# Six transpositions of x with float32r operands, from raw copies made by DMA within SBUF

## The chip, the cores and the metric

The kernel runs on one core of one Trainium2 chip. The metric is the device time of one execution in microseconds (us), the median of several executions; lower is better. The core has a matrix engine (PE, with its weight loads shown apart as PEld), three engines for element-wise work (DVE, ACT, POOL) and SP, which here issues all DMAs. Each engine works through its own queue in order and waits on semaphores for the others.

## What is computed

Three layers, in float32, for a batch of 2, a sequence of 768 and a width of 512 (8 heads of 64):

```
attn = softmax over keys of the same hash bucket of (q k^T / 8), times v     # 2 x 8 heads
x    = attn, heads side by side                                              # (2, 768, 512)
theta = x @ w_theta
y  = w_tok_r . (x cos(theta)) + w_tok_i . (x sin(theta))                     # over the sequence
u  = x + y
x  = u + relu(u @ w_ch)
out = x + relu(layernorm(x) g @ w_ch1) @ w_ch2
```

## The kernel before, in words

Every float32 product is made of float32r products: an operand is split into a high part (a cast to float32r) and a low part (the rest), and three of the four products of parts are added in PSUM.

The attention runs as 48 steps, two blocks of 128 queries each. A step ends with `pv_mm` (the product with v, line 405, tile `o`), `pv_evac_a` (ACT, line 414, tile `ot`) and `pv_evac_b` (DVE, line 423), which writes the transposed x: `XT[b]`, a tile per batch (b = 0, 1) with the width on partitions, 128 partitions by 4 by 768 words. In the listings these three are `PV`, `O` and `X`; the last of them is `X.47`. The pool of tiles that the attention used, `ap_`, is closed after it, and its place in SBUF is taken by one large tile, `arena` (128 partitions by 10 slots of 2,048 words).

The second layer works on twelve blocks of 128 tokens, named by batch b and block j. For a block, `z_h` and `z_l` split x (tiles `xh`, `xl`), `z_m` multiplies it with the split w_theta (line 790, tile `th`), `z_a` to `z_f` make cosine and sine, `z_t` transposes x back to tokens on partitions and `z_u` (ACT, line 776) takes that out of PSUM into `U`, `z_p` multiplies it with cosine and sine, and `z_q` and `z_w` split the products into `z_o[b, j]`. For j over 0, `z_o[b, j]` is slot 2j - 2 + b of `arena`, so slots 8 and 9 are those of block 5. `mix_mm` (line 856, tile `acc`) multiplies the token weights (`tokh`, `tokl`) with these, six products per step.

`z_t` (line 773, tile `xps`) is four transpositions on PE: each loads a 128 by 128 block of `XT[b]` as weights and streams the identity `ident`, both float32.

From line 505 on the order of every engine's queue is the order of the program (`manual_schedule`), and the program is written out by hand as lists of steps: `tail` (the end of the attention with the start of the second layer), then `half1`, `trans` and the rounds of the third layer. A step's arguments are numbers: `z_t.0.5.1` is block (0, 5) into PSUM bank T1, `mix.2.0` is product step 2 of batch 0, `ld.t.3.0` and `ld.c.0.1` are loads of token weights and of w_ch, issued on SP (line 106, tile `st`). The place that matters here is the end of `tail` and the start of `half1`:

```
    tail = ... PV.47 z_u.1.0 z_h.1.1 cv_y.t.1.1 z_t.1.1.1
        mix.0.0 O.47 z_r.1.0 z_u.1.1 cv_l.t.1.0.1 z_p.0.1.0 X.47
    half1 = z_u.1.3 z_c.1.0.1 z_q.0.1.0 z_f.1.0.0 z_f.1.0.1 ld.c.0.1 z_l.1.1 z_f.1.0.2 z_t.0.5.1
        mix.2.0 ... z_m.1.1.2 z_w.1.0.1.0 z_t.0.2.1 ...

    run(tail)
    actx.close()
    zq = zctx.enter_context(tc.tile_pool(name="z", bufs=1, side="right", reuse_waits="tile"))
    arena.append(zq.tile([128, 2 * NI - 2, 2048], F32R, name="arena"))
    run(half1)
```

On PE the six products of `mix.0.0` are followed at once by the four transpositions of `z_t.0.5.1`; on SP the last DMA ahead of `half1` is `ld.t.3.1`; `z_q.0.1.0` (ACT, a cast at line 94) is the first instruction that writes `arena`, into slot 0.

Of the kernel before, what the change touches and what calls it, by code (L numbers as in the profile page):

```python
# [10 lines left out]
F32R = mybir.dt.float32r  # L11
# [22 lines left out]
def attn_moe_kernel(  # L34
# [28 lines left out]
    vec, act, pool, pe, sp = nc.vector, nc.scalar, nc.gpsimd, nc.tensor, nc.sync  # L63

    def f(ap):
        return ap.bitcast(F32)
# [4 lines left out]
    def bank(tag, name):  # L71
        return psum.tile([128, 512], F32, tag=tag, name=name)
# [6 lines left out]
    ident = const.tile([128, 128], F32, name="ident")  # L79
# [8 lines left out]
    XT = {}  # L88
# [497 lines left out]
    for i in range(8):  # L586
        c, x = divmod(i, 2)
# [145 lines left out]
    def U(i):  # L733
        if i not in U_AT:
            return U0[:, i if i < 4 else i - 2, :]
        j, y = U_AT[i]
        if j not in ur:
            ur[j] = r_new(j, F32, f"u{j}")
        return ur[j][:, y, :]
# [4 lines left out]
    arena = []  # L744
# [8 lines left out]
    zb, zr, zw = {}, {}, {}  # L753
# [16 lines left out]
    def z_t(b, j, k):  # L770
        zb[b, j] = bank(f"T{k}", f"xps{b}{j}")
        for d in range(4):
            pe.transpose(zb[b, j][:, d * 128:(d + 1) * 128], XT[b][:, d, j * 128:(j + 1) * 128], ident)

    def z_u(b, j):
        act.activation(U(b * NI + j), zb.pop((b, j)), AF.Copy)

# [70 lines left out]
    def mix_mm(half, j, t, b):  # L848
        if j == 0 and t != 1:
            mix_acc(half, t, b)  # L850
        th, tl = tok_t[half, j]
        acc, z = acc_t[half, b, t], z_o[b, j]
        k = 0
        for x in range(2):
            for w, y in ((th, 0), (th, 1), (tl, 0)):
                pe.matmul(  # L856
                    acc, w[:, x, t * 128:(t + 1) * 128], z[:, x, y, :],
                    start=(j == 0 and k == 0), stop=(j == NI - 1 and k == 5),
                )
                k += 1  # L860
# [333 lines left out]
    def o_add(r, t, x0=None):  # L1194
# [6 lines left out]


    ops.update(
        z_tab=z_tab, z_h=z_h, z_l=z_l, z_t=z_t, z_u=z_u, z_m=z_m, z_a=z_a, z_k=z_k, z_r=z_r, z_c=z_c, z_f=z_f, z_p=z_p, z_q=z_q,
        z_w=z_w, mix=lambda q, b: mix_mm(q // 18, q % 18 // TH, q % TH, b), madd=mix_add, ch_new=ch_new, ch_at=ch_at, ch_ah=ch_ah, ch_al=ch_al, ch_bm=ch_bm,
        ch_br=ch_br, ch_bs=ch_bs, ln_a=ln_a, ln_b=ln_b, ln_c=ln_c, xb_new=xb_new, xn=xn_make, xb_t=xb_t, xb_e=xb_e,
        xb_a=xb_a, xb_h=xb_h, xb_l=xb_l, ld=cv_ld, cv_y=cv_y, cv_s=cv_s, cv_b=cv_b, cv_p=cv_p, cv_j=cv_j, cv_h=cv_h, cv_l=cv_l, w1_s=w1_s,
# [3 lines left out]
    def run(text, **names):  # L1211
# [15 lines left out]
    """  # L1227

    half1 = """
        z_u.1.3 z_c.1.0.1 z_q.0.1.0 z_f.1.0.0 z_f.1.0.1 ld.c.0.1 z_l.1.1 z_f.1.0.2 z_t.0.5.1  # L1230
        mix.2.0 cv_b.t.1.1 z_w.0.1.0.0 z_u.0.5 cv_h.t.1.1 z_p.1.0.1 z_p.1.0.0 z_q.1.0.1 cv_l.t.1.1.0 z_q.1.0.0
        z_q.0.1.1 cv_y.t.2.1 z_m.1.1.2 z_w.1.0.1.0 z_t.0.2.1 z_w.1.0.0.0 z_w.0.1.1.1 z_a.1.1 z_a.0.2 z_u.0.2
        z_k.1.1.0 cv_y.t.2.0
        mix.1.0 z_k.0.2.0 z_r.1.1 cv_s.t.2.0.1 z_m.0.3.1 z_c.1.1.1 z_r.0.2 z_f.1.1.1 cv_b.t.2.1 z_f.1.1.0
        z_h.1.2
# [3 lines left out]
        mix.4.0 z_p.0.2.0  # L1239
        mix.1.1 z_w.1.1.0.0 z_h.1.3 cv_s.t.3.0.1 z_q.1.1.1 z_a.0.3 z_m.1.2.2 cv_s.t.3.1.1 z_w.1.1.1.0 z_q.0.2.0  # L1240
        z_f.0.2.1 cv_h.t.2.0 z_p.0.2.1
        mix.3.1 z_q.0.2.1 cv_h.t.2.1 z_k.0.3.0 z_h.0.4 z_w.0.2.0.0 z_r.0.3 z_t.0.3.1 z_w.0.2.1.1 z_a.1.2
        z_c.0.3.0 ld.t.4.1
        mix.5.1 z_f.0.3.1 z_k.1.2.0 cv_l.t.2.1.0 z_r.1.2 cv_l.t.2.0.1 z_l.1.3 z_f.0.3.0 z_t.1.2.2
        mix.4.1
        mix.7.0 z_u.0.3 cv_y.t.3.0 z_p.0.3.1 z_u.1.2 z_c.1.2.0 cv_y.t.3.1 z_f.1.2.1 z_m.1.3.1
        mix.3.0 ld.t.4.0 cv_b.t.3.0 z_f.1.2.0 z_q.0.3.1 cv_b.t.3.1 z_l.0.4 z_f.0.3.2 z_f.1.2.2 z_p.1.2.1
# [7 lines left out]
        z_p.0.4.0 ld.t.5.1 z_q.1.3.0  # L1255
        mix.11.0 z_w.1.3.1.0 z_q.0.4.0 z_w.1.3.0.0 cv_h.t.4.0 z_a.1.4 z_w.0.4.0.1 z_k.1.4.0 z_f.0.4.1
        cv_h.t.4.1
        mix.11.1 z_p.0.4.1 z_r.1.4 z_q.0.4.1 z_t.1.4.2 cv_l.t.4.0.1 cv_y.t.5.0 cv_l.t.4.1.0 z_w.0.4.1.0 z_a.0.5
        z_h.1.5 ld.c.1.1 z_c.1.4.1
        mix.9.1 z_l.1.5 z_k.0.5.0 cv_s.t.5.0.1  # L1260
        mix.9.0 cv_s.t.5.1.1 z_r.0.5 z_u.1.4 z_f.1.4.0 cv_b.t.5.0 cv_y.t.5.1
        mix.10.1 ld.t.6.0
        mix.10.0 z_c.0.5.0 z_f.1.4.2 z_p.1.4.0 z_f.1.4.1 z_p.1.4.1 z_f.0.5.0 z_q.1.4.0 z_f.0.5.1 z_q.1.4.1
        cv_b.t.5.1 cv_h.t.5.0 ld.t.6.1 z_p.0.5.1 z_w.1.4.0.0 z_f.0.5.2 z_m.1.5.1 z_w.1.4.1.0 z_p.0.5.0
        mix.12.0 cv_h.t.5.1 z_q.0.5.1 z_t.1.5.2 z_a.1.5 cv_l.t.5.0.1 z_w.0.5.1.0 z_k.1.5.0 cv_l.t.5.1.0 z_r.1.5
        mix.12.1 cv_s.t.6.1.1 cv_y.t.6.0 z_q.0.5.0 cv_s.t.6.0.1 z_c.1.5.0 z_u.1.5 cv_y.t.6.1 cv_b.t.6.1
        mix.13.1 z_f.1.5.1 z_f.1.5.0
        mix.14.0
# [150 lines left out]
    for r in range(3, len(rounds)):  # L1419
        g = rounds[r][0] + r % 2  # L1420
        n = g + 1
        a, b, c, d = (
            (f" ld.v.{n}.0 ld.v.{n}.1", f" cv_y.v.{n}.0 cv_s.v.{n}.0.1", f" cv_p.v.{n}.0", f" cv_j.v.{n}.0") if n < NG else ("", "", "", "")
        )
# [59 lines left out]
```

## Time and profile before

| | |
|---|---|
| median of 3 runs | 663.49 us (663.41, 663.49, 665.45) |
| span of the profiled execution, first to last instruction | 662.6 us |
| PE busy | 657.1 us (99%), 3771 matmuls |
| DVE, ACT, POOL busy | 557.5, 416.4, 310.5 us |
| granted TensorE clock, mean | 1.000 |

The profile is of one execution. What it has of that execution's time is the span, which lies 0.9 us below the median; the rest lies around the first and the last instruction. A busy PE is counted from the start of a matmul to its modelled end, which overlaps the next one; the time that a matmul takes from its neighbours is read from start to start, or from the chain of waits, which cuts overlaps off.

### The profile page before, as it was taken

How to read it: one execution, taken by the hardware profiler on the slowest of the kernel's cores; microseconds unless marked ns; L12 is line 12 of the kernel's file. 1: busy time of each engine (PE TensorE's matmuls, PEld its weight loads, DVE VectorE, ACT ScalarE, POOL GpSimd, SP SyncE). 2: the span in 40 equal slices, each digit the busy share in tenths (PEclk: the TensorE clock that was granted, in tenths of full speed). 3: DMA queues.
4: the chain of work that ended last, by engine and by line, in shares of the span. 5: the costliest groups of instructions: out<-in, count | busy, mean ns of one | idle time of the engine just before them, and what ended most of it. 6: DMA issues, size and time to landing. Idle time of an engine off the chain costs nothing.

```text
span 662.6 us, 11210 instructions
## 1 busy us (share of the span) xinstructions
PE 657.1 (99%) x3771; PEld 591.7 (89%) x3771; DVE 557.5 (84%) x1002; ACT 416.4 (63%) x864; POOL 310.5 (47%) x418
## 2 busy tenths in 40 slices
PE   9999999999999999999999999999999999999998
PEld 7999999999999888888888888989998999999997
DVE  6899988999999999999888889986767686867655
ACT  7899998999999896776535544553433433343321
POOL 5887887667787644233433133434150505051400
PEclk9999999999999999999999999999999999999999
DMA  8977544475540411222422122102121121211022
GB/s 248 240 176 173 135 108 114 116 172 128 127 96 0 161 51 61 80 75 95 148 81 64 48 96 65 63 1 64 64 65 66 62 96 33 97 49 46 1 80 111
DMA packets 32374, 62.24 MB, mean 94 GB/s; under 512 B 4482, under 2 KB 11732, under 8 KB 32317
## 3 DMA queue, kind: packets, MB, share of 16 engines
q1 hardware_dynamic: 32317, 61.53, 33.1%
q8 instruction: 30, 0.49, 0.3%
q14 instruction: 27, 0.22, 0.1%
HBM read 39.98 MB, written 3.15 MB: 65 GB/s over the span
## 4 chain that ended last, share of the span: by engine, by line
PE 95%; DVE 2%; DMA 1%; SPq 1%; POOL 1%; issue 0%; ACT 0%; POOLq 0%
PE o L1191 20%; PE acc L856 15%; PE o L405 9%; PE s L332 9%; PE t L380 9%; PE Z L1148 8%; PE a L898 5%; PE v L1148 5%; PE th L790 4%; PE zy L1148 2%; PE Y L1148 2%; PE bits L286 2%; PE s L503 1%; PE xt L967 1%; PE ut L883 1%; DMA tk<-bits 1%
## 5 line engine op out<-in xcount | busy, mean ns | idle before, releaser
L1191 PE MATMUL o<-arena,hh 128*128 128x512 f32 (+1 forms) x388 | 119.1, 388 | 0.0
L367 POOL TENSOR_SCALAR pn<-p,l,M 128x768 f32<-128x768 f32 x96 | 94.6, 986 | 38.8 <-DVE l L363 25.6
L340 DVE TENSOR_REDUCE M<-s 128x1 f32<-128x772 f32 x96 | 90.9, 947 | 4.1 <-PE s L515 2.0
L101 DVE TENSOR_TENSOR ptl<-t,pth 128x512 fp32r<-128x512 f32 x144 | 90.6, 678 | 1.3 <-ACT pth L389 1.0
L356 ACT ACTIVATE p<-s,M 128x772 f32<-128x772 f32 x96 | 87.5, 912 | 2.4 <-DVE M L340 2.0
L117 POOL TENSOR_SCALAR cs<-st 128x512 f32<-128x512 f32 (+2 forms) x68 | 44.8, 665 | 84.6 <-DVE cy L131 75.1
L1191 PEld LDWEIGHTS o<-arena,hh 128*128 128x128 f32 x388 | 72.1, 188 | 13.6
L389 ACT ACTIVATE pth<-t 128x512 fp32r<-128x512 f32 x144 | 81.1, 599 | 4.3 <-PE t L380 3.0
L332 PE MATMUL s<-tk,tq 128*128 128x386 f32 (+1 forms) x360 | 82.8, 351 | 0.0
L380 PE MATMUL t<-ident,pn 128*128 128x128 f32 x576 | 80.3, 273 | 0.4 <-POOL pn L367 0.4
L1191 PE MATMUL o<-arena,hl 128*128 128x512 f32 (+1 forms) x194 | 75.5, 389 | 0.0
L856 PE MATMUL acc<-arena,tokh 128*128 128x512 f32 x240 | 75.3, 395 | 0.0
L380 PEld LDWEIGHTS t<-ident,pn 128*128 128x128 f32 x576 | 68.5, 141 | 6.3 <-POOL pn L367 1.4
L1156 ACT ACTIVATE sn<-Z 128x384 f32<-128x384 f32 x39 | 19.2, 492 | 67.2 <-PE Z L1148 67.2
L332 PEld LDWEIGHTS s<-tk,tq 128*128 128x128 f32 (+1 forms) x360 | 59.4, 190 | 0.1
L856 PEld LDWEIGHTS acc<-arena,tokh 128*128 128x128 f32 x240 | 44.0, 188 | 8.5
L1198 DVE TENSOR_TENSOR U<-o,U 128x512 f32<-128x512 f32 x48 | 32.9, 689 | 21.2 <-PE o L1191 20.5
L856 PE MATMUL acc<-arena,tokl 128*128 128x512 f32 x120 | 46.9, 391 | 0.0
L405 PE MATMUL o<-pth,vv 128*128 128x256 f32 x288 | 46.0, 295 | 0.1
L131 DVE SCALAR_TENSOR_TENSOR cy<-cy,cs 128x512 uint32<-128x512 uint32 (+2 forms) x72 | 41.4, 575 | 3.6
L114 ACT ACTIVATE cy<-st 128x512 f32<-128x512 f32 (+2 forms) x72 | 39.5, 561 | 7.8 <-DVE tokl L101 2.5
L125 DVE SCALAR_TENSOR_TENSOR cs<-st,cs 128x512 uint32<-128x512 uint32 (+2 forms) x76 | 44.1, 580 | 0.2
(260 smaller groups left out, 1481.8 us busy)
## 6 DMA issues: line engine op xcount, KB each, us to landing
st<-in_w_dram SPq DMA_DIRECT2D x36, 256.0 KB
st<-in_w_dram SPq DMA_DIRECT2D x14, 512.0 KB
tk<-hik SPq DMA_DIRECT2D x30, 193.0 KB
tq<-hiq SPq DMA_DIRECT2D x30, 192.0 KB
st<-in_wrT_dram SPq DMA_DIRECT2D x12, 384.0 KB
st<-in_wiT_dram SPq DMA_DIRECT2D x12, 384.0 KB
vs<-in_v_dram SPq DMA_DIRECT2D x8, 384.0 KB
tk<-lok SPq DMA_DIRECT2D x15, 193.0 KB
```

Source lines behind the costliest of these rows:

```text
L101: eng.tensor_tensor(out=o, in0=i, in1=f(hi), op=ALU.subtract)
L117: eng.tensor_scalar(out=s, in0=f(t)[:, :, 1], scalar1=0.0, scalar2=1.0, op0=ALU.mult, op1=ALU.mult)
L332: pe.matmul(ps[:, hf, 0:HW], lt[0:K, x * 128:(x + 1) * 128], rt[0:K, hf, :], start=(K == 128), stop=(K != 128),)
L340: vec.tensor_reduce(out=m_t[p][:, 0, i:i + 1], in_=s_ps[p, i][:, :, 0:HW], axis=AX.XY, op=ALU.max, negate=True)
L356: act.activation(pt, ps[:, :, 0:HW], AF.Exp, bias=m[:, 0, i:i + 1], accum_out=l_t[p][:, 0, i:i + 1])
L367: pool.tensor_scalar(out=pn.rearrange("p (h c) s -> p h (c s)", h=2), in0=p_t.pop((p, i))[:, :, 0:HALF], scalar1=l_t[p][:, 1, i:i + 1], sc ...
L380: pe.transpose(ps[:, w * 128:(w + 1) * 128], pn_t[p, i][:, c, :], ident)
L389: act.activation(ph, t_ps[p, u], AF.Copy)
L405: pe.matmul(ps, vv[:, c, e].rearrange("p a d -> p (a d)"), x[:, c::NI, :], start=(k == 0), stop=(k == 2 * NI - 1),)
L856: pe.matmul(acc, w[:, x, t * 128:(t + 1) * 128], z[:, x, y, :], start=(j == 0 and k == 0), stop=(j == NI - 1 and k == 5),)
L1148: pe.matmul(ps_t[r, b], W1[g][y][:, w, d, :], XB[s][x][:, z, d, :], start=(first == 1 and k == 0), stop=(k == 5), skip_group_check=True,)
L1191: pe.matmul(ps, lt[:, i * 128:(i + 1) * 128], W2[g][:, y, x, n], start=(k == 0), stop=(k == 5))
```

## The change

Six of the twelve `z_t` become `z_tx`: blocks (0, 5), (0, 2), (0, 3), (1, 2), (1, 4), (1, 5). For each, a DMA on SP (`z_x`) copies the block's words out of `XT[b]` (128 partitions, four runs of 512 bytes each) into a part of slots 8 and 9 of `arena`, whose type is float32r. The first `z_x` also copies `ident` into slot 9 on DVE as float32r. `z_tx` then makes the four transpositions with both operands float32r. All six `z_x` stand at the very start of `half1`; the `z_tx` stand where the `z_t` were. Nothing else moves.

```
+    raw_at = {(0, 5): (8, 0), (0, 2): (8, 1), (0, 3): (8, 2), (1, 2): (9, 0), (1, 4): (9, 1), (1, 5): (9, 2)}
+    tr_id = []
+
+    def z_x(b, j):
+        k, x = raw_at[b, j]
+        if not tr_id:
+            tr_id.append(arena[0][:, 9, 1536:1664])
+            vec.tensor_copy(tr_id[0], ident)
+        zw[b, j, "x"] = arena[0][:, k, 512 * x:512 * x + 512].rearrange("p (d s) -> p d s", d=4)
+        sp.dma_start(out=f(zw[b, j, "x"]), in_=XT[b][:, :, j * 128:(j + 1) * 128])
+
+    def z_tx(b, j, k):
+        zb[b, j] = bank(f"T{k}", f"xps{b}{j}")
+        x = zw.pop((b, j, "x"))
+        for d in range(4):
+            pe.transpose(zb[b, j][:, d * 128:(d + 1) * 128].bitcast(F32R), x[:, d, :], tr_id[0])
...
     half1 = """
-        z_u.1.3 z_c.1.0.1 z_q.0.1.0 z_f.1.0.0 z_f.1.0.1 ld.c.0.1 z_l.1.1 z_f.1.0.2 z_t.0.5.1
+        z_x.0.5 z_x.0.2 z_x.0.3 z_x.1.2 z_x.1.4 z_x.1.5
+        z_u.1.3 z_c.1.0.1 z_q.0.1.0 z_f.1.0.0 z_f.1.0.1 ld.c.0.1 z_l.1.1 z_f.1.0.2 z_tx.0.5.1
```

In the same way `z_t.0.2.1`, `z_t.0.3.1`, `z_t.1.2.2`, `z_t.1.4.2` and `z_t.1.5.2` become `z_tx` at their places.

## Rows read from the trace of the kernel before

**Rows 1.** The page: span, PE's busy time, and the chain by engine.

```profile
span 662.6 us, 11210 instructions
PE 657.1 (99%) x3771; PEld 591.7 (89%) x3771; DVE 557.5 (84%) x1002; ACT 416.4 (63%) x864; POOL 310.5 (47%) x418
...
PE 95%; DVE 2%; DMA 1%; SPq 1%; POOL 1%; issue 0%; ACT 0%; POOLq 0%
```

**Rows 2.** Busy time by stretch: us, then PE, PEld, DVE, ACT, POOL; clock; DMA.

```profile
225.00:245.00 20.00, 19.61 (x127) 17.30 (x126) 19.24 (x30) 17.26 (x33) 11.26 (x13) 1.00 0.32 102
245.00:310.00 65.00, 65.00 (x299) 53.64 (x298) 63.66 (x107) 46.62 (x85) 21.53 (x23) 1.00 0.23 70
310.00:480.00 170.00, 169.87 (x842) 146.31 (x841) 141.40 (x291) 78.89 (x168) 58.43 (x74) 1.00 0.22 73
```

**Rows 3.** The chain of waits, 235 to 270 us: start, us, what.

```profile
241.71 1.43 PE o L405 x12
...
244.98 0.44 PE xps L773 x4
245.41 1.38 PE acc L856 x6
246.80 2.73 PE th L790 x12
```

**Rows 4.** Timeline around z_t.0.5.1: start, us, engine, line [idle before it <- releaser].

```profile
244.14 0.68 DVE L826 TENSOR_TENSOR t<-t,U 128x512 f32<-128x512 f32 x1
...
244.81 0.60 PE L773 MATMUL xps<-ident,xT 128*128 128x128 f32 x4
244.85 0.42 DVE L423 TENSOR_TENSOR xT<-o,ot 64x256 f32<-64x256 f32 x1
...
245.30 0.63 ACT L94 ACTIVATE arena<-t 128x512 fp32r<-128x512 f32 x1 [0.34 <-DVE xT L423]
...
247.49 0.58 ACT L776 ACTIVATE u<-xps 128x512 f32<-128x512 f32 x1
```

**Rows 5.** Weight loads, timeline cut to two loads each; and all of line 773.

```profile
241.05 0.20 PEld L773 LDWEIGHTS xps<-ident,xT 128*128 128x128 f32 x2 [0.59 <-PE xps L773]
...
241.44 0.30 PEld L405 LDWEIGHTS o<-pth,vv 128*128 128x128 f32 x2
...
L773 PEld LDWEIGHTS xps<-ident,xT x48: 138/140/143, 229.0 to 301.9; 128*128 128x128 f32 x48
```

**Rows 6.** SP's DMA issues of copies within SBUF, 60 to 70 us.

```profile
61.02 0.54 SPq L248 DMA_DIRECT2D tq<-hiq  x1
...
65.44 0.95 SPq L262 DMA_DIRECT2D tk<-bits  x1
```

**Rows 7.** Stretches after those issues, after 177.32 (v) and after 246.60 (wrT), as rows 2.

```profile
61.00:62.00 1.00, 1.00 (x10) 0.96 (x10) 0.85 (x3) 1.00 (x2) 0.56 (x1) 1.00 0.00 0
...
64.00:65.00 1.00, 1.00 (x11) 1.00 (x10) 1.00 (x3) 0.95 (x4) 0.86 (x1) 1.00 0.98 204
...
178.30:179.30 1.00, 1.00 (x10) 1.00 (x9) 1.00 (x3) 1.00 (x4) 1.00 (x3) 1.00 0.57 166
...
248.00:249.00 1.00, 1.00 (x6) 0.84 (x5) 1.00 (x3) 1.00 (x4) 0.00 (x0) 1.00 0.84 283
```

**Rows 8.** Timeline: SP's issues of token weights and w_ch, and POOL's first reader.

```profile
234.83 0.42 SPq L106 DMA_DIRECT2D st<-in_w_ch_dram  x1
246.60 0.33 SPq L106 DMA_DIRECT2D st<-in_wrT_dram  x1
...
254.85 0.65 POOL L117 TENSOR_SCALAR cs<-st 128x384 f32<-128x384 f32 x1 [1.16 <-DVE cy L131]
```

**Rows 9.** PE's first matmuls, timeline.

```profile
1.30 4.00 PE L549 MATMUL warm<-pb_lo 128*128 128x384 f32 x12 [1.30 <-DVE pb_lo L545]
...
5.83 0.34 PE L286 MATMUL bits<-hik,pb_hi 128*128 128x384 f32 x1
6.00 0.34 PE L286 MATMUL bits<-lok,pb_lo 128*128 128x384 f32 x1
```

More of the change, by code (lines that the diff above doesn't have):

```diff
@@ L1203, in attn_moe_kernel @@
     ops.update(
-        z_tab=z_tab, z_h=z_h, z_l=z_l, z_t=z_t, z_u=z_u, z_m=z_m, z_a=z_a, z_k=z_k, z_r=z_r, z_c=z_c, z_f=z_f, z_p=z_p, z_q=z_q,
+        z_tab=z_tab, z_h=z_h, z_l=z_l, z_t=z_t, z_x=z_x, z_tx=z_tx, z_u=z_u, z_m=z_m, z_a=z_a, z_k=z_k, z_r=z_r, z_c=z_c, z_f=z_f, z_p=z_p, z_q=z_q,
         z_w=z_w, mix=lambda q, b: mix_mm(q // 18, q % 18 // TH, q % TH, b), madd=mix_add, ch_new=ch_new, ch_at=ch_at, ch_ah=ch_ah, ch_al=ch_al, ch_bm=ch_bm,
@@ L1229, in attn_moe_kernel @@
     half1 = """
-        z_u.1.3 z_c.1.0.1 z_q.0.1.0 z_f.1.0.0 z_f.1.0.1 ld.c.0.1 z_l.1.1 z_f.1.0.2 z_t.0.5.1
+        z_x.0.5 z_x.0.2 z_x.0.3 z_x.1.2 z_x.1.4 z_x.1.5
+        z_u.1.3 z_c.1.0.1 z_q.0.1.0 z_f.1.0.0 z_f.1.0.1 ld.c.0.1 z_l.1.1 z_f.1.0.2 z_tx.0.5.1
         mix.2.0 cv_b.t.1.1 z_w.0.1.0.0 z_u.0.5 cv_h.t.1.1 z_p.1.0.1 z_p.1.0.0 z_q.1.0.1 cv_l.t.1.1.0 z_q.1.0.0
-        z_q.0.1.1 cv_y.t.2.1 z_m.1.1.2 z_w.1.0.1.0 z_t.0.2.1 z_w.1.0.0.0 z_w.0.1.1.1 z_a.1.1 z_a.0.2 z_u.0.2
+        z_q.0.1.1 cv_y.t.2.1 z_m.1.1.2 z_w.1.0.1.0 z_tx.0.2.1 z_w.1.0.0.0 z_w.0.1.1.1 z_a.1.1 z_a.0.2 z_u.0.2
         z_k.1.1.0 cv_y.t.2.0
@@ L1241, in attn_moe_kernel @@
         z_f.0.2.1 cv_h.t.2.0 z_p.0.2.1
-        mix.3.1 z_q.0.2.1 cv_h.t.2.1 z_k.0.3.0 z_h.0.4 z_w.0.2.0.0 z_r.0.3 z_t.0.3.1 z_w.0.2.1.1 z_a.1.2
+        mix.3.1 z_q.0.2.1 cv_h.t.2.1 z_k.0.3.0 z_h.0.4 z_w.0.2.0.0 z_r.0.3 z_tx.0.3.1 z_w.0.2.1.1 z_a.1.2
         z_c.0.3.0 ld.t.4.1
-        mix.5.1 z_f.0.3.1 z_k.1.2.0 cv_l.t.2.1.0 z_r.1.2 cv_l.t.2.0.1 z_l.1.3 z_f.0.3.0 z_t.1.2.2
+        mix.5.1 z_f.0.3.1 z_k.1.2.0 cv_l.t.2.1.0 z_r.1.2 cv_l.t.2.0.1 z_l.1.3 z_f.0.3.0 z_tx.1.2.2
         mix.4.1
@@ L1257, in attn_moe_kernel @@
         cv_h.t.4.1
-        mix.11.1 z_p.0.4.1 z_r.1.4 z_q.0.4.1 z_t.1.4.2 cv_l.t.4.0.1 cv_y.t.5.0 cv_l.t.4.1.0 z_w.0.4.1.0 z_a.0.5
+        mix.11.1 z_p.0.4.1 z_r.1.4 z_q.0.4.1 z_tx.1.4.2 cv_l.t.4.0.1 cv_y.t.5.0 cv_l.t.4.1.0 z_w.0.4.1.0 z_a.0.5
         z_h.1.5 ld.c.1.1 z_c.1.4.1
@@ L1264, in attn_moe_kernel @@
         cv_b.t.5.1 cv_h.t.5.0 ld.t.6.1 z_p.0.5.1 z_w.1.4.0.0 z_f.0.5.2 z_m.1.5.1 z_w.1.4.1.0 z_p.0.5.0
-        mix.12.0 cv_h.t.5.1 z_q.0.5.1 z_t.1.5.2 z_a.1.5 cv_l.t.5.0.1 z_w.0.5.1.0 z_k.1.5.0 cv_l.t.5.1.0 z_r.1.5
+        mix.12.0 cv_h.t.5.1 z_q.0.5.1 z_tx.1.5.2 z_a.1.5 cv_l.t.5.0.1 z_w.0.5.1.0 z_k.1.5.0 cv_l.t.5.1.0 z_r.1.5
         mix.12.1 cv_s.t.6.1.1 cv_y.t.6.0 z_q.0.5.0 cv_s.t.6.0.1 z_c.1.5.0 z_u.1.5 cv_y.t.6.1 cv_b.t.6.1
```

## The prediction

> **What bounds the kernel now.** I read the page first. PE is busy for 657.1 of a span of 662.6 us, and 95% of the chain that ended last is PE [rows 1]. Then busy time by stretch: from 245 to 310 us, where the changed transpositions stand, and on to 480, PE has hardly an idle microsecond, while ACT and POOL have many [rows 2]. So from here on the end of the kernel moves with PE: what PE saves is saved, and what PE waits is lost, since nothing later on PE is waiting for another engine and could give the loss back. Before 245 this is not so clean: PE lacks 0.4 us between 225 and 245, DVE only 0.8. Third, the chain of waits from 235 to 270, which gives what PE's work costs from neighbour to neighbour: a set of four transpositions 0.44 us, so 0.11 each; six products of 512 columns 1.38, so 0.23 each; twelve float32r products of 256 columns 1.43, so 0.12 each [rows 3]. The chain counts from end to end, so its times lie some 0.17 us behind the starts in the timeline. Last, the timeline around the first changed set [rows 4]: this shows what happens on the other engines at the very time when PE reaches it.
>
> **What the change saves.** Six sets change. A float32r matmul of 256 columns takes 0.119 us and one of 512 takes 0.228 [rows 3], so 128 columns more cost 0.055 and a matmul of 128 columns would take 0.065. The float32 one takes 0.109. But each transposition also loads its own 128 columns of weights, and loads have a pace of their own. Two float32 transposition loads, the first after a wait of 0.59 us, last 0.14 each and 0.20 together, so they start 0.06 apart; two loads for float32r products, behind a set of transpositions, last 0.19 each and 0.30 together, so 0.11 apart [rows 5]. So today matmuls pace a set, not loads. The new form, a transposition of float32r words, is not in the trace. Bounds: at best it takes 0.065 throughout, 0.26 a set, a saving of 0.18 a set and 1.1 us in all; at worst it runs like the float32r products of 256 columns, 0.119 each, a loss of 0.035 a set and 0.2 us in all. I take the transposition's load as it is now (0.06 apart), since it is still a transposition, and the matmul as float32r (0.065); the product behind the set still needs its own load, 0.11 behind the last transposition's start. Then a set takes 3 x 0.065 + 0.11 = 0.305, a saving of 0.135, and six sets **save 0.8 us**.
>
> **What the change makes PE wait for.** The first copy, `z_x.0.5`, writes `arena`. That tile lies where the attention's tiles lay. The first writer of `arena` today is ACT's cast into slot 0; its operand was ready at 244.82 (line 826), ACT stood idle, and what released it at 245.30 was the DVE instruction of line 423, 244.85 + 0.42 = 245.27 [rows 4]. That is `X.47`, the end of the attention, which neither makes that operand nor uses slot 0. So a first write to `arena` waits for the whole of the attention, and `z_x.0.5` will too, although its source has been complete for long. PE reaches the set of block (0, 5) at 244.81 [rows 4], before `X.47` has even begun. The sum, from 245.27:
> - SP sees the semaphore and issues: at least the 0.03 that ACT needed; I take 0.07 (up to 0.15).
> - The copy lands. SP's group of eight copies within SBUF [rows 6] is the nearest row for its kind: issued at 61.02, no bytes move until 62.0, and then the engines move some 200 GB/s at a share of 0.98 [rows 7]. The copy has 262 KB, so 1.0 + 1.3, with an allowance of 0.3 for completion: 2.6 us. Lower bound: 283 GB/s, as the load issued at 246.60 reaches, and no allowance, 1.9. Upper bound: 166 GB/s, as the load of v in runs of 512 bytes shows in its first stretch, and an allowance of 0.6, 3.2 [rows 7].
> - PE takes the semaphore and loads the first block: 0.06 to 0.11 for the load [rows 5]; I take 0.1.
>
> PE starts the set at 245.27 + 0.07 + 2.6 + 0.1 = 248.04 instead of 244.81: **PE waits 3.2 us**, bounds 2.5 and 3.9. Nothing covers it: all that follows on PE is queued behind this set.
>
> **The rest of the change.** The copy of the identity runs on DVE right behind `X.47`. No row has its shape; it lies between nothing and the 0.42 of line 423 [rows 4], and ends before the first copy lands, so it costs nothing; the subtraction behind it makes `xl` for matmuls that move by 3.2 us. The other five copies: the second set stands behind the first one, six and twelve products, 0.44 + 1.38 + 2.73 later [rows 3], so at 252.6 with the wait, and even six copies at 200 GB/s are done 1.0 + 7.9 us after 245.34, in the order of their sets, the second by some 249.3; no further wait. On SP, `ld.c.0.1` (issued at 234.83) and `ld.t.3.0` (246.60) now stand behind the six issues [rows 8]. Among the eight copies the seventh issue comes 4.4 us after the first [rows 6], so these two leave at about 249.8 and 250.2, their bytes queue behind the copies until 254.2 and take 2.4 more at 283 GB/s [rows 7]; `ld.t.3.0` lands near 256.7. Its first reader, on POOL, starts at 254.85 [rows 8], moved to 258.05: it holds by 1.4 us. `ld.c.0.1` has its first reader in the list behind `mix.15.0`. ACT takes the set out of PSUM at 247.49 [rows 4] and will do so near 249; what is queued behind it on ACT comes 1.5 us late, for PE work that comes 3.2 late. So none of these takes over the bound.
>
> **Sum.** +3.2 - 0.8 = +2.4 us, or +0.36%. I carry the 0.9 us between span and median over unchanged: 663.49 + 2.4 = **665.9 us**. About 0.3% (2.0 us) is what a measurement of this kernel tells from no change. With the bounds, 2.5 - 1.1 = +1.4 to 3.9 + 0.2 = +4.1, 664.9 to 667.6.
>
> **Rivals.**
> - *The copies come in time.* If `arena`'s wait were kept by region, or `z_x.0.5` could otherwise be issued by 242.1 (2.7 before 244.81), PE would never wait, and only the saving is left: 662.7 us, not slower, within 0.3%. SP is free from 234.83 + 0.42 on, and the source is old. Against it stands ACT's cast, which waited for `X.47` without sharing a byte with it. Chance 0.08.
> - *No faster transposition.* If the load of float32r words keeps the 0.11 of a float32r load, a set still takes 0.44, and only the wait is left: 666.7 us. For it: the new weights have the type whose loads show 0.11. Against it: today's transposition load at 0.06, with the same number of words. The Trainium skill, page "TensorE: Matmul & The Clock Gate", section "LDWEIGHTS (loading the stationary operand)", states that a load takes its number of columns divided by 1.2 in nanoseconds, whatever else it is, 107 for 128 columns; by that rule nothing could be saved. The float32r loads agree with it, the transposition's loads 0.06 apart do not [rows 5]. Chance 0.25.
> - *The clock falls in the wait.* The stretches read are at a granted clock of 1.00, the 2.4 GHz level, and have no idle of 3 us [rows 2]. At the kernel's start, after idling, twelve matmuls of 384 columns take 4.00 us, 0.33 each, the 1.2 GHz level; soon after, two start 0.17 apart [rows 9]. If PE resumes like that and stays so for as long, some 3.6 us, eleven matmuls' worth lose 0.16 each: 1.7 us, so 667.6 us, or 668.4 without the saving. The Trainium skill, on the same page, section "Why this matters for your kernels", warns that idle gaps between bursts of matmuls bring the lower level back; no run here shows a gap of this size within the kernel. Chance 0.15.
>
> **How the numbers follow.** The forecast has 0.48, the rivals 0.08, 0.25 and 0.15; 0.04 is left for what I don't see, such as a late token weight. The forecast's own sum stays under +2.0 in about one case of six, so slower by over 0.3% has 0.40 + 0.25 + 0.15 = 0.80; within 0.3% has 0.08 + 0.08 + 0.01 = 0.17; faster 0.03, since even the best saving without any wait is 1.1 us. The range goes from 664.5, just under the forecast's lower bound, to 668.5, the clock's case without the saving; outside it lie the copies in time and the worst mixtures, less than 2 in 10.
>
> **What would show it.** Right: SP issues the first copy close behind line 423's last instruction; PE's first new set starts near 248 with an idle of about 3 us, released by a DMA; the other five sets have no idle before them; a set takes about 0.3 us in the chain; the granted clock stays 1.00. Wrong: an issue before 245, an idle under 2 us, sets of 0.44, a stretch at the lower clock, or new idle before `acc` or `th` that a late token weight or ACT ends.

## The result: 669.4 us instead of 664.5, and the profile after

| | before | after |
|---|---|---|
| median, same series of runs | 664.47 us (663.41 to 666.24, 4 executions) | 669.4 us (667.2 to 670.5, 4 executions) |
| ratio of the two | | 1.007, 95% interval 1.0045 to 1.0095 |
| span of the profiled execution | 662.6 us | 665.4 us |
| its granted TensorE clock, mean | 1.000 | 1.000 |

The change makes the kernel slower by 0.7%, more than the forecast 0.36%. The time of an execution is its span and 1.8 us, so the profiled execution of after is the shortest of the four, 667.2 us; the mean clocks of the others are 0.997, 0.997 and 0.995.

Lines of the second and third layer stand 17 later in the changed kernel: the new transpositions are L790, the products `acc` L873, `th` L807. The engines' busy time on the page of after, as in [rows 1]:

```profile
PE 657.7 (99%) x3771; PEld 592.3 (89%) x3771; DVE 556.6 (84%) x1003; ACT 417.3 (63%) x864; POOL 309.4 (46%) x418
```

On the page hardly anything has moved: PE's busy time is the same within 0.6 us, and the span has grown by 2.8. So PE does the same work and waits somewhere. The chain of waits of after, here from 244 to 254 us (start, us, what), says where; it answers to [rows 3]:

```profile
244.34 0.43 DVE xT L423
244.77 0.02 issue
244.79 2.62 DMA arena<-xT
247.41 0.14 issue
247.54 0.51 PE xps L790 x4
248.05 1.43 PE acc L873 x6
...
252.21 0.29 PE xps L790 x4
252.51 1.46 PE acc L873 x6
```

A chain that in the kernel before ran on PE here leaves it: from the first new set it goes back to the copy, and from the copy to the end of `X.47` (line 423). The timeline of after, 243 to 251 us (start, us, engine, line, [idle before it <- releaser]), shows the same place as [rows 4] with SP's issues:

```profile
244.29 0.40 PE L873 MATMUL acc<-z,tokl 128*128 128x512 f32 x1
244.34 0.42 DVE L423 TENSOR_TENSOR xT<-o,ot 64x256 f32<-64x256 f32 x1
244.79 4.25 SPq L784 DMA_DIRECT2D arena<-xT  x6
244.80 0.23 DVE L782 CAST arena<-ident 128x128 fp32r<-128x128 f32 x1
244.80 0.63 ACT L94 ACTIVATE arena<-t 128x512 fp32r<-128x512 f32 x1 [0.38 <-DVE xT L423]
...
247.54 0.51 PE L790 MATMUL xps<-arena 128*128 128x128 f32 x4 [2.86 <-DMA arena<-xT]
...
249.08 0.65 SPq L106 DMA_DIRECT2D st<-in_w_ch_dram  x1
...
249.84 0.40 SPq L106 DMA_DIRECT2D st<-in_wrT_dram  x1
```

Line 423 ends at 244.76. SP's first copy, DVE's identity cast and ACT's cast, all first writes to `arena`, start at 244.79 and 244.80. PE's last product starts at 244.29 and products start 0.23 apart, so PE is free at 244.52 and begins the set at 247.54: a wait of 3.0 us. (The 2.86 in brackets counts from the modelled end of that product.)

What a set costs is read from the timeline, from its start to the start of the product behind it, without overlaps. The second set, which waits for nothing, before:

```profile
249.36 0.60 PE L773 MATMUL xps<-ident,xT 128*128 128x128 f32 x4
249.72 0.70 PE L856 MATMUL acc<-z,tokh 128*128 128x512 f32 x2
```

and after:

```profile
252.05 0.46 PE L790 MATMUL xps<-arena 128*128 128x128 f32 x4
252.34 0.70 PE L873 MATMUL acc<-z,tokh 128*128 128x512 f32 x2
```

The set takes 0.36 us before and 0.29 after. The chain has 0.44 and 0.29 for it, but there the six products behind it grow from 1.39 to 1.46 as well, and set and products together shrink from 1.82 to 1.75. Either way a set saves some 0.07. The last of the changed sets starts here, before and after:

```profile
301.70 0.60 PE L773 MATMUL xps<-ident,xT 128*128 128x128 f32 x4
```

```profile
303.96 0.45 PE L790 MATMUL xps<-arena 128*128 128x128 f32 x4
```

From the start of the first set to there PE takes 56.89 us before (from 244.81 [rows 4]) and 56.42 after (from 247.54): with small idle times between them, six sets save about 0.45.

So in the execution with a full clock the wait less the saving is 3.0 - 0.45 = 2.55, but the span is 2.8 longer. The rest is found in the third layer, after:

```profile
558.71 0.56 DVE L1180 TENSOR_TENSOR c<-v,sn 128x384 f32<-128x384 f32 x1 [0.75 <-ACT arena L94]
...
558.96 0.34 PE L1165 MATMUL Z<-xb,arena 128*128 128x384 f32 x1
...
559.32 0.30 PEld L1165 LDWEIGHTS v<-xb,w1h 128*128 128x128 f32 x2 [0.35 <-DVE c L1180]
```

and before:

```profile
556.64 0.34 PE L1148 MATMUL Z<-xb,arena 128*128 128x384 f32 x1
...
556.81 0.51 PE L1148 MATMUL v<-xb,w1h 128*128 128x384 f32 x2
```

After, PE waits for a sum on DVE that it did not wait for before. The product `v` starts 0.36 behind the one ahead of it instead of 0.17, and with the next start 0.30 us are lost in all. So most of what the six sets save is gone again: from the start of the first set to the start of PE's last product (661.85 after, 659.17 before) it is 414.31 us after and 414.36 before. The profiles of a_after, b_fill, c_five, d_later and f_halffill, whose sets are new as well, have the same wait of 0.35; those of before, e_before, g_wait and i_copies, whose sets are all float32, don't, and neither does j_early. Why DVE comes later there is open. What this doesn't give is the median, 4.9 above the kernel before.

### The profile page after: what moved, and what is told of

It reads as the page before. It is cut to its first block, busy times and chain, and to the rows that moved or that the text cites. A ratio compares the mean times of both kernels' runs of the same rounds, so it can differ in the third digit from the quotient of the medians.

```text
span 665.4 us, 11222 instructions
## 1 busy us (share of the span) xinstructions
PE 657.7 (99%) x3771; PEld 592.3 (89%) x3771; DVE 556.6 (84%) x1003; ACT 417.3 (63%) x864; POOL 309.4 (46%) x418
## 4 chain that ended last, share of the span: by engine, by line
PE 94%; DVE 4%; DMA 1%; issue 0%; ACT 0%; SPq 0%; DVEq 0%
PE o L1208 20%; PE acc L873 15%; PE o L405 9%; PE t L380 8%; PE s L332 8%; PE Z L1165 8%; PE a L915 5%; PE v L1165 5%; PE th L807 5%; PE zy L1165 2%; PE Y L1165 2%; PE bits L286 2%; DVE M L340 1%; DVE ptl L101 1%; PE s L503 1%; PE xt L984 1%
## 5 line engine op out<-in xcount | busy, mean ns | idle before, releaser
L873 PE MATMUL acc<-arena,tokh 128*128 128x512 f32 x240 | 75.3, 395 | 0.0
L873 PEld LDWEIGHTS acc<-arena,tokh 128*128 128x128 f32 x240 | 44.0, 188 | 8.5
L873 PE MATMUL acc<-arena,tokl 128*128 128x512 f32 x120 | 46.9, 391 | 0.0
```

The lines of the kernel that those rows point to most:

```text
L873: pe.matmul(acc, w[:, x, t * 128:(t + 1) * 128], z[:, x, y, :], start=(j == 0 and k == 0), stop=(j == NI - 1 and k == 5),)
```

## The experiments

Two theories stood at first. *Wait alone*: the loss is the wait less the saving, and what lies above that is chance. *Wait and clock*: PE's idleness brings its clock down as well, and that costs a part of its own. A third, *more work on the queues*, puts the rest on the copies and the loads behind them. Each experiment that changes the kernel starts from the changed one unless it says otherwise.

**a_after: the changed kernel again**, without an edit, for more executions and a second profile.

> The changed kernel again, as the measure for the others. Clock theory (the wait of 3.0 us lets PE's clock fall in most executions): executions spread from about +2 us over the kernel before (mean granted clock 1.000) to +6 us (mean clock 0.995 to 0.997), the median near +4 to +5. Rival (the clock is not the cause, the spread is that of any kernel here): time and mean granted clock of the executions do not go together, or the kernel before shows the same spread of clocks.

Measured: 668.66 us (666.65 to 670.42, 6 executions) against 664.19 (23 executions), ratio 1.0068 [1.0052, 1.0084]. The profiled execution, of 669.45 us, has a mean clock of 0.997. Busy time by stretch (us, PE, PEld, DVE, ACT, POOL; clock; DMA) shows where that is from (rows of 3.3 and 3.4 us):

```profile
248.90:252.20 3.30, 3.30 (x9) 2.62 (x8) 2.09 (x4) 2.88 (x6) 0.79 (x1) 0.50 1.11 336
252.40:255.80 3.40, 3.40 (x19) 2.80 (x18) 1.26 (x3) 0.96 (x2) 0.86 (x2) 1.00 0.28 107
```

and PE's timeline there:

```profile
248.23 0.51 PE L790 MATMUL xps<-arena 128*128 128x128 f32 x4 [3.08 <-DMA arena<-xT]
248.57 0.95 PE L873 MATMUL acc<-z,tokh 128*128 128x512 f32 x2
...
251.02 0.63 PE L807 MATMUL th<-thh,xh 128*128 128x512 f32 x1
...
251.87 0.57 PE L807 MATMUL th<-thh,xl 128*128 128x512 f32 x1
252.28 0.39 PE L807 MATMUL th<-thh,xh 128*128 128x512 f32 x1
```

PE comes back from its wait at full pace, and from 248.9 on the granted clock is 0.50, the 1.2 GHz level: products of 512 columns start 0.43 apart, until 252.28. The six products of `acc` and the first three of `th` take 3.71 us from start to start (252.28 - 248.57), and at 0.23 each they would take 2.05: a loss of 1.7 us. Over both batches of the changed kernel, eight of ten executions have a mean clock under 0.998. The two without average 666.9 us, the six at 0.997 average 668.9, the two at 0.995 are at 670.4 and 670.5. The steps of 2.0 and 3.5 us are about the size of one such stretch and of two.

**g_wait: the wait alone.** Only the first copy is left, with no identity cast, and all sets are float32 again; the first one reads the copy.

```
-            pe.transpose(zb[b, j][:, d * 128:(d + 1) * 128].bitcast(F32R), x[:, d, :], tr_id[0])
+            pe.transpose(zb[b, j][:, d * 128:(d + 1) * 128], f(x[:, d, :]), ident)
...
-        z_x.0.5 z_x.0.2 z_x.0.3 z_x.1.2 z_x.1.4 z_x.1.5
+        z_x.0.5
```

> The wait by itself: all twelve sets float32 as before, but that of block (0, 5) reads a float32 copy made by one DMA at the same place; no float32r identity, no other copy. Wait and clock theory: PE idle of about 3 us at 244.8, mean clock 0.995 to 0.997 in most executions, and 0.9 us (six savings) over the changed kernel: some +5.4 us over the kernel before in the median, +3.1 in an execution without a fall. Rival (copies and float32r sets carry a part of the loss): clearly less than the changed kernel's +4.5 us.

Measured: 668.53 us (667.8 to 670.57, 6 executions) against 664.67, ratio 1.0064 [1.005, 1.0077]; five of the six are under 0.998. Its chain has "DMA arena<-xT" of 2.61 us from 245.41 and the set at 248.16, and the stretches of the profiled execution (668.8 us of span) have the lower level twice as long:

```profile
245.00:247.00 2.00, 0.10 (x1) 0.00 (x0) 1.93 (x4) 1.67 (x5) 0.41 (x1) 1.00 0.10 31
247.20:254.00 6.80, 5.84 (x16) 4.82 (x17) 3.58 (x6) 3.51 (x7) 1.84 (x2) 0.50 0.35 116
254.00:262.00 8.00, 8.00 (x38) 6.63 (x38) 6.19 (x12) 4.03 (x8) 1.27 (x2) 1.00 0.18 49
```

One copy, without the other five and without float32r, costs 3.9 us by the medians, within the intervals the same as the whole change. Wait and clock carry the loss. In the profiled execution the set and what follows it up to the next set take 7.32 us (248.16 to 255.48) instead of 4.55, so this longer stretch costs 2.8. The expected +5.4 added 0.9 for six savings that the changed kernel was to have and g_wait not; it did not come, which agrees with a saving that hardly reaches the end. Nor does every single execution fit: two at 0.997 took 667.8, no longer than the one at 1.000 (667.92).

**i_copies: the copies alone.** All six copies and the cast are issued and nothing reads them; all sets are float32 again, as `z_t`, at their places. (One of six such lines:)

```
-        z_u.1.3 ... z_f.1.0.2 z_tx.0.5.1
+        z_u.1.3 ... z_f.1.0.2 z_t.0.5.1
```

> The copies by themselves: the six DMAs and the identity's copy on DVE stay, but all twelve sets read x and the float32 identity as before, so nothing waits for the copies. Wait theory: as the kernel before, within 0.3 us. Rival (copies cost beyond the wait, by the DVE copy, SP's later loads or DMA traffic): 0.5 us or more slower, with new idle of PE behind 245 us.

Measured: 664.69 us (663.75 to 665.2, 11 executions) against 664.67, ratio 1.0000 [0.9992, 1.0009]. SP issues as in the changed kernel:

```profile
245.11 4.25 SPq L784 DMA_DIRECT2D arena<-xT  x6
249.40 0.65 SPq L106 DMA_DIRECT2D st<-in_w_ch_dram  x1
250.16 0.39 SPq L106 DMA_DIRECT2D st<-in_wrT_dram  x1
```

Their 1.5 MB, the cast on DVE and the loads of token weights and w_ch held back on SP cost nothing. *More work on the queues* falls.

**c_five: five sets of six.** Block (0, 5) is back on `z_t`, without a copy; the other five stay new.

```
-        z_x.0.5 z_x.0.2 z_x.0.3 z_x.1.2 z_x.1.4 z_x.1.5
-        z_u.1.3 ... z_f.1.0.2 z_tx.0.5.1
+        z_x.0.2 z_x.0.3 z_x.1.2 z_x.1.4 z_x.1.5
+        z_u.1.3 ... z_f.1.0.2 z_t.0.5.1
```

> The changed kernel, with block (0, 5) alone back to the float32 transpositions from x itself and without its copy: five sets stay float32r. Wait theory: no wait at 244.8, mean clock 1.000, and five savings of 0.15 us: 0.7 to 0.8 us faster than the kernel before. Rival (the copies cost something beyond that wait): no faster than before, or an idle of PE at another set.

Measured: 664.75 us (663.1 to 665.12, 11 executions) against 664.19, ratio 1.0004 [0.9995, 1.0013]. Its chain of waits:

```profile
243.52 0.44 PE xps L773 x4
243.96 1.38 PE acc L873 x6
245.34 2.73 PE th L807 x12
248.07 0.30 PE xps L790 x4
```

The chain stays on PE, no set waits, all clocks lie between 0.999 and 1.000, and the whole loss is gone. The first set's wait is the only thing in the change whose cost shows in the time. The gain of the other five sets, some 0.35 us by the reading above or 0.05%, does not: the lower end of the interval just reaches it, and its middle lies at no gain. The profile has the wait for DVE in the third layer, and from the start of the set of block (0, 5) to the start of PE's last product it takes 414.48 us, the kernel before 414.36 and, in e_before's profile, 414.45. The 0.7 to 0.8 us that were expected did not come.

**b_fill: the wait filled.** Behind the products of `mix.0.0`, thirteen products of 512 columns on old data run into the PSUM bank of the set, which then overwrites them; they are more work, and the set still has to wait for the copy.

```
     def z_tx(b, j, k):
         zb[b, j] = bank(f"T{k}", f"xps{b}{j}")
+        if (b, j) == (0, 5):
+            for _ in range(13):
+                pe.matmul(zb[b, j], TA["h"][:, 0, 0:128], TA["h"][:, 1, :], start=True, stop=True)
```

> The changed kernel, with 13 products of 512 columns that nobody reads put ahead of the set of block (0, 5) on PE: 13 x 0.227 = 2.95 us of work in place of the idle wait; nothing is left out. Clock theory: the clock stays at its upper level in every execution (mean 1.000), and the time falls from that of the changed kernel by some 2 to 3 us in the median, to about +2.2 us over the kernel before: more work, less time. Rival (the extra time beyond the wait comes from the copies' traffic, from late loads or from other engines): the same time as the changed kernel within 0.5 us, or slower.

Measured: 667.24 us (666.97 to 668.23, 5 executions) against 664.19, ratio 1.0051 [1.0039, 1.0063], every clock 0.999 or 1.000. In its chain the copy still lands before the set (first fence), and the stretches (second fence) have the full level throughout:

```profile
245.32 2.62 DMA arena<-xT
...
248.08 0.51 PE xps L793 x4
```

```profile
245.00:247.00 2.00, 2.00 (x10) 1.65 (x10) 1.93 (x5) 1.67 (x4) 0.32 (x1) 1.00 0.15 46
248.20:251.60 3.40, 3.40 (x18) 2.85 (x18) 2.64 (x5) 2.98 (x6) 0.33 (x1) 1.00 1.17 346
```

Thirteen products more, the set no earlier, and 1.4 us less than a_after beside it on the same chip. That is less than the 2 to 3 expected, and the two intervals overlap a little, so the medians alone would not settle it. The clocks do: none of five executions is under 0.998 here, five of six are in a_after. The second stretch has eighteen matmuls, where a_after had nine in about the same time. That is the clock's part, shown by taking it away: without the idle time the level stays, and 3.05 us of the loss remain, which is the wait with hardly any saving.

**f_halffill: the wait half filled**, with six of those products instead of thirteen.

> The changed kernel with 6 of the 13 filling products ahead of the set of block (0, 5): 1.36 us of the wait is filled, some 1.7 us stay idle, and PE goes on at the same time as in the changed kernel. Clock theory, if the length of the idle stretch matters: few or no executions below a mean clock of 0.999, median near that of the full filling, 667.2 us. If any idle of this kind makes the clock fall: as the changed kernel, about 668.7 us, with most mean clocks at 0.995 to 0.997.

Measured: 667.7 us (666.31 to 670.68, 6 executions) against 664.67, ratio 1.0055 [1.0036, 1.0073]; four of the six clocks are 1.000, one is 0.997 and one, the profiled execution, 0.995. PE's timeline and two stretches of it:

```profile
246.24 1.52 PE L791 MATMUL xps<-thh 128*128 128x512 f32 x6
249.46 0.51 PE L793 MATMUL xps<-arena 128*128 128x128 f32 x4 [1.71 <-DMA arena<-xT]
```

```profile
11.20:14.50 3.30, 3.30 (x18) 3.30 (x17) 3.30 (x6) 2.99 (x8) 3.04 (x5) 0.50 1.07 327
250.00:253.40 3.40, 3.40 (x9) 2.63 (x9) 2.23 (x4) 3.02 (x6) 0.74 (x1) 0.51 1.17 350
```

PE's last filler starts near 247.4, so it idles from 247.6 to 249.46, 1.9 us. After that idle time too the level fell, in this execution for certain and in at most two of the six. The other stretch, at 11 us, has nothing to do with the change: it lies near the kernel's start. So a mean of 0.997 in an execution without a profile is no proof of a fall in the wait; what is, is the count (below). The 667.7 lies between the two times expected, 667.2 and 668.7.

**e_before: the kernel before against itself**, for the spread.

> The kernel before under another name (one empty line more): the measure for the spread and for a second trace of it. Expected: ratio 1.000 within 0.1%, spread 663 to 666 us, most executions with a mean granted clock of 0.999 or 1.000. If c_five's missing 0.7 us is the luck of the one trace read so far, this trace shows other idle ahead of 245 us or behind 320 us than that one; if c_five pays for its copies, this trace agrees with the first one and c_five stands apart.

Measured: 664.23 us (663.52 to 666.19, 12 executions) against 664.67 (663.43 to 666.15, 23 executions), ratio 0.9996 [0.9987, 1.0005]. Single executions differ by 2.7 us, and four of those 23 have a clock of 0.997, as three of the 23 in the other batch. So without any wait about one execution in seven has it, which agrees with a fall at the kernel's head as the profiles of f_halffill and j_early (0.50 from 11.3 to 14.7 us) show one; where it lay in these wasn't profiled. With the wait it is 8 of 10 and 5 of 6, though some of these may have it at the head; with the wait filled 0 of 5. Where no set waits for a copy it is 0 of 22 (c_five, i_copies), 1 of 12 (d_later), 2 of 12 (j_early) and 1 of 12 (e_before).

**d_later: the first set moved back** by two rounds and into bank T2, so that its copy has landed, with its `z_u` moved along.

```
-        z_u.1.3 z_c.1.0.1 z_q.0.1.0 z_f.1.0.0 z_f.1.0.1 ld.c.0.1 z_l.1.1 z_f.1.0.2 z_tx.0.5.1
+        z_u.1.3 z_c.1.0.1 z_q.0.1.0 z_f.1.0.0 z_f.1.0.1 ld.c.0.1 z_l.1.1 z_f.1.0.2
...
-        mix.0.1 z_f.1.1.2 z_p.1.1.1 cv_b.t.2.0
-        mix.5.0 ld.t.3.0 z_f.0.2.0 z_p.1.1.0 z_f.0.2.2 z_l.1.2 z_q.1.1.0
+        mix.0.1 z_f.1.1.2 z_p.1.1.1 cv_b.t.2.0 z_tx.0.5.2
+        mix.5.0 ld.t.3.0 z_f.0.2.0 z_p.1.1.0 z_u.0.5 z_f.0.2.2 z_l.1.2 z_q.1.1.0
```

> The changed kernel, with the set of block (0, 5) and its evacuation moved some 9 us later on PE and ACT, behind product step 0 of batch 1 (bank T2), so that its copy has landed; the copies stay where they are. Wait theory: no wait, mean clock 1.000, six savings of 0.15 us: 0.9 us faster than the kernel before. Rival (the copies cost something beyond that wait, or the moved evacuation delays ACT): no faster than before, with new idle on PE that ACT or a load ends.

Measured: 664.56 us (663.19 to 666.53, 12 executions) against 664.19, ratio 1.0009 [1.0001, 1.0018]. The wait for the copy is gone and another has come, as PE's timeline shows:

```profile
250.71 0.39 PE L873 MATMUL acc<-z,tokl 128*128 128x512 f32 x1
251.45 0.50 PE L807 MATMUL th<-thh,xh 128*128 128x512 f32 x1 [0.35 <-ACT U L793]
```

PE is free at 250.94 and waits 0.5 us until ACT has taken a set out of PSUM in line 793: what is late next is ACT, with its other work of `half1` queued ahead of that. The new wait is as long as what six sets save, and the wait for DVE in the third layer is there as well: the 0.9 us expected did not come.

**j_early: the first copy out of `arena`.** It gets a tile of its own in a pool that is open all along, with its identity, cast on POOL, and is issued in `tail`; the other five stay.

```
-            tr_id.append(arena[0][:, 9, 1536:1664])
-            vec.tensor_copy(tr_id[0], ident)
-        zw[b, j, "x"] = arena[0][:, k, 512 * x:512 * x + 512].rearrange("p (d s) -> p d s", d=4)
+            xe = mp.tile([128, 640], F32R, name="xe")
+            tr_id.append(xe[:, 512:640])
+            cast(pool, tr_id[0], ident)
+            y = xe[:, 0:512]
+        else:
+            y = arena[0][:, k, 512 * x:512 * x + 512]
+        zw[b, j, "x"] = y.rearrange("p (d s) -> p d s", d=4)
...
-        z_t.0.1.1 z_tab cv_b.t.0.1 z_a.0.0 ...
+        z_t.0.1.1 z_tab z_x.0.5 cv_b.t.0.1 z_a.0.0 ...
```

> The changed kernel with the copy for block (0, 5) and the float32r identity in a small tile of the mixing pool, which is free early, in place of arena; that copy is issued in the tail, some 15 us earlier, and the identity's copy runs on POOL there. The other five copies stay. Arena theory (the first copy waited for the end of the attention because it writes arena, not for its operand): the copy is issued before 240 us, no idle of PE at 244.8, mean clock 1.000, all six sets float32r at 0.29 us: 0.5 to 0.9 us faster than the kernel before. Rival (the copy waits for something else, such as its source as a whole or the queue): issued at 245 us again, the same wait of 3 us and about 668.7 us.

Measured: 664.9 us (663.7 to 667.25, 12 executions) against 664.76, ratio 1.0003 [0.9991, 1.0014]. SP's issues of copies (first fence) and its chain of waits (second fence):

```profile
222.76 0.72 SPq L788 DMA_DIRECT2D xe<-xT  x1
...
246.97 3.47 SPq L788 DMA_DIRECT2D arena<-xT  x5
```

```profile
244.82 0.44 PE xps L773 x4
245.25 1.40 PE acc L877 x6
246.65 0.29 PE xps L794 x4
```

The first new set follows its products at once, in 0.29 us. Its copy left at 222.76, with the attention still running; the five copies that still go to `arena` are issued from 246.97 on, after `X.47`. What held the first copy back was the place it was written to, not its source and not SP, which in the changed kernel is free from 234.83 (234.50 + 0.33) to 244.79. Six new sets without a wait, and still no gain that the times show: 0.45 us is 0.07%, within an interval of 0.9991 to 1.0014, which of the 0.5 to 0.9 us expected allows 0.6 at most. In the profile PE takes 56.71 us from the first set to the last, only 0.18 less than before, and 414.23 to its last product. No version here beats the kernel before.

## Why the prediction was right and wrong

- **The bound and the place: right for the wait.** PE sets the end, and what it waits at block (0, 5) is lost; g_wait and c_five show it from both sides. That "what PE saves is saved", since nothing later on PE waits, was read from stretches that end at 480 us [rows 2]; at 559 us PE waits for DVE once the sets are faster, and that takes 0.30 back.
- **The wait: right.** Start of the set 2.77 us behind the end of `X.47` forecast, 2.78 measured (247.54 - 244.76). Issue after 0.03 instead of 0.07, landing 2.62 instead of 2.6, start 0.14 behind it instead of 0.1. PE came to the set 0.24 us ahead of the end of `X.47`, where the trace of before has 0.46, hence 3.0 instead of 3.2. The reason, a first write to `arena` that waits for the whole attention [rows 4], is shown by j_early.
- **No further wait: right.** The other five sets have no idle before them, `ld.c.0.1` and `ld.t.3.0` leave at 249.08 and 249.84 where 249.8 and 250.2 stood, and i_copies shows that all of this is free.
- **The saving: mis-sized.** "A saving of 0.135, and six sets **save 0.8 us**" measured about 0.07 and 0.45, of which 0.05 is left at PE's last product. The set itself came out as forecast, 0.29 against 0.305, and so the rival *no faster transposition* falls; its parts came out otherwise (the starts lie 0.06, 0.06, 0.08 and 0.09 apart, not three times 0.065 and 0.11), so the agreement is partly luck. What was wrong was the number it was taken from: 0.44 is the chain's, from end to end, while 0.305 was built from start to start. From start to start the old set took 0.36. The text said that the chain's ends lie behind the starts and then subtracted across the two.
- **The clock: the failed step.** "The stretches read are at a granted clock of 1.00": the forecast let it stay so, with 0.15 for the rival *the clock falls in the wait*. By the mean clocks it fell in most executions (8 of 10 in the changed kernel), and in a_after's profile that cost 1.7 us, the rival's price; the longer stretch of g_wait's cost 2.8. The rival's time of 667.6 us carried the saving of 0.8 and a low base (next point). The two executions without a fall, 667.2 and 666.65, lie 2.7 and 2.5 us above the kernel before in their own series. With 2.7 and one fall, 664.47 + 2.7 + 1.7 = 668.9; the median of four is 669.4, above the range's end of 668.5. The forecast of 2.4 for the case without a fall is near those two by errors that offset each other: the wait was taken 0.2 too long, and the saving that reaches the end far too large.
- **The base: a term that was off by chance.** The sum starts from 663.49, the median of three executions. Four gave 664.47, and the batches beside the runs 664.19, 664.67 and 664.76. The 0.9 between span and median is no property of an execution: by the 1.8 that every execution here has, the one profiled before took 664.4.
- **Why 0.15 was too low.** [Rows 9] show that PE, idle before its first products, begins at the lower level, and the expected wait was 3.2 us with nothing on PE. Against that stood only that no row had such a gap in it, which is no reason against it. The Trainium skill, "TensorE: Matmul & The Clock Gate", section "Why this matters for your kernels", warned that idle gaps bring the lower level back; the stretch at 0.50 in a_after and the filled wait of b_fill bear that out. The Trainium skill's rule on the duration of a load, on the same page, section "LDWEIGHTS (loading the stationary operand)", is columns divided by 1.2 in nanoseconds, so 107 for 128 columns. It is not borne out as the pace of these loads: four transpositions of float32r words, each with a load of its own, and the product behind them start within 0.29 us (252.05 to 252.34), where four such loads would take 0.43 by an estimate from the Trainium skill's figure on that page.

## What to carry to other kernels

A transfer that an otherwise full matrix engine has to wait for costs its wait and, often, a stretch at half pace behind it: price both, and fill the gap with products that nobody reads if it can't be removed. A tile that is laid over the place of closed ones is not free when its own slots are; put what is needed early somewhere that was never shared. Subtract durations only when both are read in the same way, from start to start. And follow a small saving to the last stretch of the kernel: here 0.45 us were gained by 304 us, and 0.30 of them were gone again at 559.

## What the runs showed of the hardware

- The lower level came after PE had been idle for some 3 us in the midst of a stretch that was full before and after (in one execution of f_halffill after 1.9 us), and not at once: in a_after the set and a product ran at full pace first, while in g_wait the level fell at 247.2, before PE was back at 248.16. It lasted 3.4 us there and 6.8 us here, and then returned while PE was busy.
- More products took less time: b_fill, with thirteen more, ran 1.4 us faster than a_after by the medians, with intervals that overlap a little, and kept a clock of 0.999 or 1.000 in all five executions.
- A copy of 256 KB within SBUF in runs of 512 bytes lands 2.6 us after its issue, and SP needs 0.7 us for each issue (six in 4.25 us).
